# A four-layer attention stack, its instructions placed by a list scheduler at build time and its scores made in 64-row tiles

## The chip, the cores and the metric

The kernel runs on one core of a Trainium2 chip. The metric is the device time of one execution in microseconds (us).

The engines are PE (TensorE, matmuls), PEld (its weight loads), DVE (VectorE), ACT (ScalarE), POOL (GpSimd) and SP (SyncE, which here only issues DMAs). "Granted clock" is the share of the full TensorE clock that the throttle let through.

## The reference, cut to what matters

Two kinds of layer alternate, A, B, A, B, on 2048 tokens of width 512 with 32 heads of width 16. Each has a layer norm in front and adds its result to x.

```python
# A: four segments of 512 tokens, causal softmax inside a segment, a memory M between segments
for s in range(4):
    logits = einsum('bhqd,bhkd->bhqk', qs, ks) * scale + mask
    a_dot  = einsum('bhqk,bhkd->bhqd', softmax(logits), vs)
    a_mem  = einsum(phi(qs), M) / (einsum(phi(qs), z) + 1e-6)
    outs.append(g * a_mem + (1 - g) * a_dot)
    M = M + einsum('bhld,bhle->bhde', phi(ks), vs)      # z likewise
# B: linear attention; phi_q, phi_k = [softmax(p), softmax(-p)] over 16 features
kv  = einsum('bhsf,bhsd->bhfd', phi_k, v)               # over ALL 2048 tokens
o   = einsum('bhqf,bhfd->bhqd', phi_q, kv) / den
# x + A(norm(x)), x + B(norm(x)), and both once more
```

The exponentials of A's scores are the largest piece of ACT's work. And B needs the sum over all tokens before its first query, so every B layer is a barrier, where one layer drains and the next one fills.

## The kernel before: the parts that the argument touches

Work is written as Python generators, and the order is made by hand: a main generator yields, and fillers are advanced by one step at each yield.

```python
def run_pipelined(main_gen, fillers):
    fi = 0
    for _ in main_gen:
        if fillers:
            g = fillers[fi % len(fillers)]
            try: next(g)
            except StopIteration: fillers.remove(g)
            fi += 1
    # ... the rest of the fillers is drained
```

Scores are made for a pair of heads. The keys of the pair stand in a masked copy (KTm, one of four per group of eight heads), the queries in another (Qblk, even and odd heads). Each score has 512 or 256 columns and lies in one of three one-bank PSUM buffers.

```python
def st_and_exp(m, jset=(0, 1, 2, 3)):          # inside a_att
    g, sl = pairs[m]
    for j in jset:                              # key block
        i = j
        while i < 4:                            # query blocks i, i+1
            nb = min(2, 4 - i)
            stbuf = self.ST[st_i % self.NST]    # NST = 3
            self.mm(stbuf[:, 0:nb * 256], self.KTm[:, g, sl, j * 128:(j + 1) * 128],
                    self.Qblk[b][:, g, i:i + nb, :, :], ...)      # 128 rows
            self.act(dst, stbuf[:, 0:nb * 256]..., ACT.Exp, scale=0.25, ...)
            # the diagonal block is masked by POOL, 128x256
            i += nb
# ... 17-column PV matmuls per head, DVE copies PVsb and NMsb out of PSUM, combined later
```

The softmax here doesn't subtract the row's maximum and nothing guards it: scores larger than these inputs give would overflow.

## Time and profile before

| kernel before | |
|---|---|
| time, median of 4 (lowest to highest) | 1223.22 us (1220.18 to 1225.22) |
| granted clock, mean of the profiled run | 0.762 |
| columns of score exponentials | 512 x 512 and 256 x 256 |

The first part of the page of the kernel before gives, for each engine, its busy time, its share of the span and its number of instructions:

```profile
PE 741.9 (61%) x5659; PEld 352.0 (29%) x5760; DVE 649.0 (53%) x1345; ACT 495.1 (40%) x1034; POOL 355.9 (29%) x734
```

The second part of the page cuts the span into 40 slices. A digit is the busy share in tenths, and PEclk is the granted clock in tenths:

```profile
PE   0577766757675674454447687676667567445544
...
DVE  2635553446544535547787535445654353454766
ACT  0288445424553560122103785552456356113110
...
PEclk9989785767677776676667798887878786667776
```

No engine is above 61%, and only 3 of the 40 slices show a 7 or more on PE and on ACT at once. The chain of waits, followed back from the last instruction, changes engines all the time:

```profile
PE 37%; DVE 33%; ACT 14%; issue 7%; POOL 4%; DMA 3%; SPq 2%; DVEq 0%; POOLq 0%; ACTq 0%
```

The list of waits of the kernel before (who waited, for whom, us in all, times, longest) shows the hand-offs of the attention loop:

```profile
POOL PT L240 <- ACT PT L235: 334.8, 290, 12.3
...
PEld ST L220 <- ACT PT L235: 166.5, 360, 5.9
...
ACT PT L235 <- PE ST L220: 120.4, 54, 12.5
```

The table by stage (stretch, its length, busy us of PE, PEld, DVE, ACT and POOL with their counts, granted clock, DMA share, GB/s) shows one stretch of attention and two around B's queries:

```profile
90.00:190.00 100.00, 72.51 (x617) 35.73 (x627) 57.21 (x119) 60.98 (x131) 28.68 (x71) 0.84 0.07 14
480.00:560.00 80.00, 37.52 (x182) 15.60 (x186) 45.83 (x95) 13.57 (x24) 19.49 (x30) 0.65 0.09 19
560.00:660.00 100.00, 52.01 (x311) 24.95 (x314) 73.29 (x140) 20.24 (x32) 33.16 (x32) 0.67 0.15 28
```

Around B's queries ACT is busy a fifth of the time and PE about half. The groups of instructions (line, engine, operation, names and shapes, count, then busy us and mean ns of one, then idle us before them and what ended it) give the score loop. The lines are those of three helpers: L220 issues every matmul, L235 every ACT instruction, L240 every DVE and POOL one.

```profile
L235 ACT ACTIVATE PT<-ST 128x512 bf16<-128x512 f32 x512 | 286.3, 612 | 152.8 <-PE ST L220 120.4 <-PE KV L220 13.6 <-PE ATT L220 10.3
L240 POOL TENSOR_SCALAR_AFFINE_SELECT PT<-PT 128x256 bf16<-128x256 bf16 x512 | 205.1, 417 | 335.1 <-ACT PT L235 334.8
L220 PE MATMUL ST<-Qblk,AREA 128*128 128x512 bf16 x459 | 190.8, 462 | 42.1 <-DVE AREA L240 22.1 <-ACT PT L235 16.5 <-issue 1.5
```

The mean time of one is longer than the distance between two starts, so starts are the better cost. Taken from the trace, back-to-back starts of 512-column exponentials are 0.476 us apart (mean time 0.612), of 512-column matmuls 0.215 (mean time 0.462), of 17-column matmuls 0.025.

### The profile page before, as it was taken

How to read it: one execution, taken by the hardware profiler on the slowest of the kernel's cores; microseconds unless marked ns; L12 is line 12 of the kernel's file. 1: busy time of each engine (PE TensorE's matmuls, PEld its weight loads, DVE VectorE, ACT ScalarE, POOL GpSimd, SP SyncE). 2: the span in 40 equal slices, each digit the busy share in tenths (PEclk: the TensorE clock that was granted, in tenths of full speed). 3: DMA queues.
4: the chain of work that ended last, by engine and by line, in shares of the span. 5: the costliest groups of instructions: out<-in, count | busy, mean ns of one | idle time of the engine just before them, and what ended most of it. 6: DMA issues, size and time to landing. Idle time of an engine off the chain costs nothing.

```text
span 1222.7 us, 16010 instructions
## 1 busy us (share of the span) xinstructions
PE 741.9 (61%) x5659; PEld 352.0 (29%) x5760; DVE 649.0 (53%) x1345; ACT 495.1 (40%) x1034; POOL 355.9 (29%) x734
## 2 busy tenths in 40 slices
PE   0577766757675674454447687676667567445544
PEld 0243332323232331122222243232323233213222
DVE  2635553446544535547787535445654353454766
ACT  0288445424553560122103785552456356113110
POOL 1053221214222431123430343231323153112433
PEclk9989785767677776676667798887878786667776
DMA  6010100001000000101210100000000000010112
GB/s 207 17 19 1 23 15 16 1 5 31 18 1 1 19 19 9 27 5 22 39 31 17 28 1 9 10 18 1 14 9 14 1 18 19 5 31 1 43 43 52
DMA packets 79024, 26.23 MB, mean 21 GB/s; under 512 B 70752, under 2 KB 78944, under 8 KB 78944
## 3 DMA queue, kind: packets, MB, share of 16 engines
q1 hardware_dynamic: 74528, 21.01, 8.4%
q10 hardware_dynamic: 4416, 4.20, 1.0%
q8 instruction: 45, 0.74, 0.3%
q14 instruction: 35, 0.29, 0.1%
HBM read 6.32 MB, written 2.10 MB: 7 GB/s over the span
## 4 chain that ended last, share of the span: by engine, by line
PE 37%; DVE 33%; ACT 14%; issue 7%; POOL 4%; DMA 3%; SPq 2%; DVEq 0%; POOLq 0%; ACTq 0%
PE GEN L220 13%; PE KV L220 9%; ACT PT L235 8%; PE ST L220 7%; PE ATT L220 6%; DVE den L240 3%; ACT AREA L235 3%; DVE stats L240 3%; DVE Zk L240 2%; DVE Qblk L240 2%; DVE PVsb L240 2%; DVE AREA L240 2%; ACT Ek L235 2%; DVE Vt L240 2%; POOL rstd L240 2%
## 5 line engine op out<-in xcount | busy, mean ns | idle before, releaser
L235 ACT ACTIVATE PT<-ST 128x512 bf16<-128x512 f32 (+1 forms) x768 | 337.6, 547 | 152.8 <-PE ST L220 120.4
L220 PE MATMUL ST<-Qblk,AREA 128*128 128x512 bf16 (+1 forms) x715 | 256.6, 409 | 91.8 <-ACT PT L235 54.3
L240 POOL TENSOR_SCALAR_AFFINE_SELECT PT<-PT 128x256 bf16<-128x256 bf16 x512 | 205.1, 417 | 335.1 <-ACT PT L235 334.8
L220 PEld LDWEIGHTS ST<-Qblk,AREA 128*128 128x128 bf16 x768 | 77.0, 103 | 227.6 <-ACT PT L235 166.5
L220 PEld LDWEIGHTS ATT<-VT,PT 128*128 128x128 bf16 x2560 | 109.2, 101 | 56.3 <-issue 20.9
L220 PE MATMUL ATT<-VT,PT 128*128 128x17 bf16 x2560 | 107.9, 174 | 11.1 <-POOL PT L240 10.9
L240 DVE CAST PVsb<-ATT 128x136 bf16<-128x136 f32 x128 | 37.7, 294 | 136.7 <-PE ATT L220 128.4
L220 PE MATMUL ATT<-MSb,PhiQT 128*128 128x34 bf16 x384 | 26.8, 187 | 98.4 <-DVE PVsb L240 98.4
L220 PE MATMUL KV<-Vt,Ek 128*128 128x136 bf16 x256 | 41.1, 308 | 58.0 <-DVE KV L240 25.2
L240 DVE TENSOR_REDUCE Zk<-Ek 128x64 f32<-128x1024 bf16 x32 | 39.0, 1218 | 48.9 <-ACT Ek L235 48.9
L240 POOL CAST Vt<-rZk 128x32 bf16<-128x32 f32 x64 | 20.4, 318 | 140.5 <-DVE Vt L240 140.5
L235 ACT ACTIVATE AREA<-GEN,S 128x512 bf16<-128x512 f32 x44 | 30.2, 687 | 75.9 <-PE GEN L220 75.1
L235 ACT ACTIVATE Ek<-GEN 128x512 bf16<-128x512 f32 x40 | 23.9, 597 | 84.7 <-PE GEN L220 82.8
L220 PE MATMUL GEN<-xnT,WA_q 128*128 128x512 bf16 x87 | 31.5, 503 | 42.3 <-DMA xnT<-xn_tile 42.1
L240 POOL TENSOR_SCALAR rstd<-mv 128x4 f32<-128x4 f32 x16 | 3.6, 228 | 179.3 <-DVE mv L240 179.3
L235 ACT ACTIVATE AREA<-GEN 128x512 bf16<-128x512 f32 x44 | 25.5, 595 | 72.4 <-PE GEN L220 71.6
L235 ACT ACTIVATE phitmpb<-GEN 128x512 bf16<-128x512 f32 x34 | 20.3, 596 | 78.7 <-PE GEN L220 56.6
L240 DVE CAST NMsb<-ATT 128x136 bf16<-128x136 f32 x96 | 28.8, 300 | 39.9 <-PE ATT L220 39.9
L220 PE MATMUL GEN<-WA_o,oT 128*128 128x512 bf16 x88 | 35.1, 538 | 22.5 <-DMA oT<-o_tile 22.0
L220 PE MATMUL GEN<-WB_o,oT 128*128 128x512 bf16 x79 | 33.1, 563 | 24.3 <-DVE dz L240 10.8
L220 PEld LDWEIGHTS ATT<-MSb,PhiQT 128*128 128x128 bf16 x384 | 16.8, 101 | 107.4 <-DVE PVsb L240 107.4
L240 DVE TENSOR_SCALAR AREA<-GEN,S 128x512 bf16<-128x512 f32 x44 | 32.7, 749 | 26.1 <-ACT AREA L235 25.0
(168 smaller groups left out, 1296.2 us busy)
## 6 DMA issues: line engine op xcount, KB each, us to landing
X<-in_A_x_dram SPq DMA_DIRECT2D x4, 512.0 KB, 9.8
out_dram<-X ACTq DMA_DIRECT2D x16, 128.0 KB, 1.7
NMsb<-in_B_wqkv_dram ACTq DMA_DIRECT2D x2, 512.0 KB, 7.0
xnT<-xn_tile SPq DMA_TRANSPOSE x64, 2.4
oT<-o_tile SPq DMA_TRANSPOSE x64, 2.4
WA_q<-in_A_wq_dram SPq DMA_DIRECT2D x1, 512.0 KB, 10.1
WB_v<-in_B_wqkv_dram ACTq DMA_DIRECT2D x1, 512.0 KB, 11.0
WA_k<-in_A_wk_dram SPq DMA_DIRECT2D x1, 512.0 KB, 12.6
```

What stands on the lines that cost most here:

```text
L220: e.matmul(o, l, r, start=st, stop=sp, tile_position=tp), reads=reads, writes=writes)
L235: return e.activation(o, i, f, scale=s, **kw)
L240: return getattr(e, m)(*a, **k)
```

## The change

The kernel is rewritten. Every instruction, or small bundle of them, becomes a node with a duration and its reads and writes, and buffers become pools. At build time a list scheduler places the nodes: a backward pass gives each node a latest start, a forward pass lets every engine take the most urgent ready node that gets its buffers, and this is repeated for some rounds. The order is then fixed in the program, with semaphores for what crosses engines. The op set changes too. The scores of eight heads and one query block are two matmuls of 512 columns on 64 rows each, in a two-bank buffer, followed by one exponential of 1024 columns. The scheduler's model counts the two score matmuls one after the other, at full clock (2 x 214 ns), so the order is planned for serial scores. The core of the diff, cut:

```diff
-def run_pipelined(main_gen, fillers):  ...      # and all generators
+class Graph:
+    def backward(self, fin): ...                 # latest starts -> priorities
+    def forward(self, prio, pools):
+        # ... events in order of model time
+            for e in ENGS:
+                while ready[e]:
+                    pr, i = heapq.heappop(ready[e])
+                    o = self.ops[i]
+                    if can_alloc(o):
+                        pick = o
+                        break
+                    skipped.append((pr, i))
+    def schedule(self, pools, rounds=4):
+        prio = [float(o.id) for o in self.ops]
+        for r in range(rounds):
+            mk = self.forward(prio, pools)       # the best round is kept
+            prio = self.backward([o.end for o in self.ops])
...
-    self.mm(stbuf[:, 0:nb * 256], self.KTm[:, g, sl, j * 128:(j + 1) * 128], rhs, ...)
-    self.act(dst, stbuf[:, 0:nb * 256]..., ACT.Exp, scale=0.25, ...)
+    self.mm(lambda S=S, KT=KT, Q4=Q4, j=j: [
+        (S.t[:, hf * 512:(hf + 1) * 512], KT.t[64 * hf:64 * hf + 64, j * 128:(j + 1) * 128],
+         Q4.t[64 * hf:64 * hf + 64, :, i * 128:(i + 1) * 128], True, True) for hf in range(2)],
+        [512] * 2, [KT, Q4], [S], opens=[PT, PV], label="S")
+    self.act(lambda PT=PT: PT.t[:], lambda S=S: S.t[:], ACT.Exp, 1024, [S], [PT], scale=0.25)
...
+ # queries spread over four slots by DMA, so that a slot holds every fourth row:
+ self.dma(lambda: [(Q4.t[sl::4, sl, :], QT.t[sl::4, :]) for sl in range(4)], 4, [QT], [Q4])
+ # PhiK by a transposing DMA, in place of a second K projection;
+ # B's keys made transposed, then turned by 64 transposing DMAs; norms by Ln and Exp on ACT
```

## The prediction

> **What bounds it now.** No engine does. The page gives PE 61%, DVE 53%, ACT 40%, POOL 29% of 1222.7 us, and the chain of work that ended last passes between them: PE 37%, DVE 33%, ACT 14%, issue 7%. The list of waits shows hand-offs: POOL's masks wait 334.8 us for exponentials, exponentials 120.4 us for scores, weight loads for scores 166.5 us for exponentials (three one-bank buffers). The table by stage shows the worst stretches around the linear-attention queries: 480-660 us and 1060-1222 us have ACT at 10-20% and PE near 50%. Granted clock is 0.762 (view by core). Its hand-made interleaving bounds it.
>
> **What the change does, with starts measured back to back in the trace.**
> - Exponentials of scores: 512 of 512 columns (0.476 us apart) and 256 of 256 (about 0.26) become 320 of 1024. From the slope, 0.83 ns per column plus 0.05, one is 0.90 us (estimate): 311 -> 289 us.
> - All ACT: 384 x 0.90 + 100 of 512 x 0.48 [...]: about 415 us.
> - Scores: 640 matmuls of 512 columns on 64 rows, against 512 of 512 plus 256 of 256: the same 137 us if serial (0.215 each), about 70 if the two row tiles overlap. [...]
> - PV stays 2560 matmuls of 17 columns (0.025 us). The second K projection, 384 narrow memory matmuls and the DVE copies PVsb and NMsb (66 us), the even/odd masks (48), KTm's ACT and DVE copies (about 90) and Zk reductions (39) go. Added: 128 DMAs that spread queries, 88 more transposing DMAs on SP (now 2.4 us to landing), 128 POOL masks of 1024 columns (about 1.1 us each, estimate) for 512 at 0.417.
> - Totals for the new kernel (estimates by count): ACT 415, PE 410-480 at full clock plus switches, DVE about 400 (before 649), POOL 150, SP issue about 350 us.
>
> **Critical path.** The attention phase of each layer needs about 192 us of ACT and 170-200 us of PE, which run side by side; a list scheduler with right durations should reach 80-85%: 230-245 us each. Around them: start until first scores about 35 us (now 61), the layer boundary 40 us, the end about 70 us (16 tiles of DVE work at about 2.1 us plus the chain). Sum 605-635; plus loss, as the order is fixed while DMA landings and the PE clock vary. I predict 655 us, range 580 to 770.
>
> **What would show it.** ACT's share near 63%, PE near 65-70%, DVE 60%; ACT digits of 8-9 in the attention phases, low only at start, middle and end; chain led by ACT and PE; score matmul pairs starting together if row tiles overlap[...]; granted clock above 0.8.
>
> **What would make it wrong.** [...] at half clock PE needs over 800 us and bounds everything. SP's queue, in order with about 360 DMAs, blocking on a late operand. Two double-bank score buffers shared with B. [...]
>
> Chances: faster 0.96, same 0.02, slower 0.02.

All of ACT came to about 415 us with a term for the norms' small instructions, where the two terms give 394 (384 x 0.90 + 100 x 0.48). And a loss at each change of tile mode, of an assumed size, was said to cancel the gain of overlapping row tiles; "switches" in PE's total are these changes. The sum, 35 + 2 x (230 to 245) + 40 + 70 = 605 to 635 us, and the 655 were made with these terms. What the traces show of the rest:

- In the new kernel the masks of 1024 columns took 1.117 us each, where 1.1 was estimated, and pairs of scores start 3 to 4 ns apart.
- The small instructions of its norms start at least 0.185 us (Ln) and 0.092 us (Exp) before the next one, and a change of tile mode costs 0.08 to 0.10 us (below).
- SP's DMA issues took 380 us in all, where about 350 was estimated; SP's queue waited for a late operand for up to 13.9 us at a time. The DMAs on the pools p landed 1.7 to 6.4 us after their issue.
- The clock records of both kernels are all either full or half. In the new kernel 512-column matmuls on 128 rows start 0.216 us apart at full and 0.427 at half. "Over 800 us" at half clock is twice the 410 to 480 of PE's total, an estimate.

## The result, and the profile after

| | before | after |
|---|---|---|
| median of 4 (lowest to highest), us | 1223.22 (1220.18 to 1225.22) | 676.38 (672.14 to 677.56) |
| ratio (95% interval) | | 0.5525 (0.5507 to 0.5544) |
| granted clock, profiled run | 0.762 | 0.863 |

A ratio is the mean time of one kernel's runs over that of the other's of the same rounds, so it is not quite the ratio of the medians quoted. Executions over 1.5% slower than the fastest of the same kernel are left out of the means. The prediction, 655 us with a range of 580 to 770, held.

The busy times of the new kernel, first part of its page:

```profile
PE 533.6 (79%) x5621; PEld 269.3 (40%) x5696; DVE 434.2 (64%) x905; ACT 448.0 (66%) x625; POOL 148.8 (22%) x143
```

Its 40 slices:

```profile
PE   0677978888988889857996666789888988996685
...
DVE  7498866347644338689999622665466633676987
ACT  3678888787977885401764466899788889752040
...
PEclk9989989779967769987999665889797975898799
```

Busy time fell too: ACT went from 495 to 448 us, PE from 742 to 534, DVE from 649 to 434, POOL from 356 to 149. The sum of these four fell by 30%, from 2242 to 1565 us; the span fell by 45%, or 547 us. So part of the gain is less work, and part is that the engines now work at the same time: on average 1.83 of the four were busy before and 2.32 are after, and ACT and PE both show mostly 7 to 9 through the two attention phases (24 of the 40 slices have 7 or more on both). Two valleys of ACT are left: the 16th to the 24th slice, around the boundary between the first pair of layers (A and B, pair 0) and the second (pair 1), and the end. The chain still changes engines, but led by two:

```profile
PE 40%; ACT 23%; DVE 22%; DMA 6%; SPq 3%; issue 3%; POOL 1%; DVEq 0%
```

The lines of waits that answer to those before. POOL's wait is now harmless idleness (22% busy); the other two are smaller:

```profile
POOL p L810 <- ACT p L504: 431.2, 117, 101.6
ACT p L504 <- PE D L498: 109.2, 71, 29.1
PEld D L498 <- ACT p L504: 83.7, 135, 2.0
```

The groups of the score loop, new kernel (L498 issues every matmul, L504 every ACT function, L810 the masks; D is the pool of two-bank PSUM buffers, G that of one-bank ones, p stands for pools of SBUF buffers):

```profile
L504 ACT ACTIVATE p<-D 128x1024 bf16<-128x1024 f32 x384 | 372.0, 1033 | 110.9 <-PE D L498 109.2
L810 POOL TENSOR_SCALAR_AFFINE_SELECT p<-p 128x1024 bf16<-128x1024 bf16 x128 | 142.4, 1117 | 431.2 <-ACT p L504 431.2
L498 PE MATMUL D<-pQ,p 64*128 64x512 bf16 x640 | 140.9, 463 | 32.2 <-ACT p L504 30.0 <-DVE p L958 0.8 <-ACT p L511 0.3
```

The exponential of 1024 columns takes 1.033 us in the mean, and back-to-back starts are 0.903 us apart, which is the predicted 0.90. The next view is the table by stage, cut at the first and last score of each layer: attention of layer pair 0, the boundary, attention of pair 1, the end.

```profile
29.00:250.00 221.00, 184.63 (x2108) 88.82 (x2134) 134.44 (x306) 186.23 (x261) 70.24 (x63) 0.85 0.24 46
250.00:351.00 101.00, 86.11 (x755) 48.63 (x762) 85.39 (x163) 42.39 (x74) 1.09 (x1) 0.93 0.36 67
351.00:580.00 229.00, 181.88 (x2065) 86.63 (x2090) 121.58 (x269) 179.31 (x235) 70.41 (x64) 0.80 0.22 45
580.00:676.00 96.00, 73.06 (x678) 41.99 (x687) 76.61 (x128) 28.51 (x34) 0.68 (x1) 0.94 0.35 78
```

In attention ACT and PE are both at about 78 to 84%; in the boundary DVE and PE are both at 85%, at the end DVE is at 80% and PE at 76%. The granted clock is 0.85 and 0.80 in attention, where it counts, and higher in between. A timeline of PE in the new kernel (start, us, instructions merged) shows a pair of scores between matmuls of 17 and of 8 columns:

```profile
123.76 0.81 PE L498 MATMUL G<-pV,p 128*128 128x17 bf16 x24
124.51 0.39 PE L498 MATMUL D<-pQ,p 64*128 64x512 bf16 x2
124.83 0.18 PE L498 MATMUL G<-MSb,p 128*128 128x8 bf16 x1
```

The two of a pair start 3 to 4 ns apart, so the row tiles do overlap. A change of tile mode costs time: from a pair to a 17-column matmul the median start-to-start time is 0.319 us where two 512-column matmuls on 128 rows are 0.216 apart, and from a 17-column matmul to a pair it is 0.105 where two 17-column matmuls are 0.025 apart. That is 0.08 to 0.10 us per change, and the trace has 406 changes.

The phases, taken from the first and last score matmul of each A layer in the one profiled run of each kernel, in us:

| kernel | start | attention 0 | boundary | attention 1 | end | clock in attention 0, 1 |
|---|---|---|---|---|---|---|
| predicted | 35 | 230 to 245 | 40 | 230 to 245 | 70 | |
| new kernel | 29.4 | 221.0 | 100.8 | 228.3 | 95.6 | 0.846, 0.798 |
| e1 | 28.8 | 263.1 | 102.5 | 290.3 | 98.2 | 0.745, 0.633 |
| e2 | 28.9 | 209.5 | 102.1 | 219.6 | 96.7 | 1.000, 0.953 |
| e3 | 29.8 | 223.5 | 103.0 | 233.8 | 96.2 | 0.855, 0.803 |
| e4 | 39.0 | 260.9 | 117.9 | 249.3 | 102.9 | 0.819, 0.807 |
| e5 | 34.6 | 211.1 | 100.6 | 225.4 | 89.4 | 0.992, 0.985 |
| e6 | 30.3 | 225.0 | 101.5 | 235.7 | 97.5 | 0.992, 0.949 |
| e7 | 29.0 | 211.2 | 93.4 | 227.0 | 98.3 | 0.950, 0.835 |
| e8 | 30.2 | 232.8 | 98.3 | 246.9 | 89.4 | 0.890, 0.807 |
| e10 | 33.6 | 216.0 | 90.2 | 213.1 | 96.7 | 0.976, 0.984 |
| e11 | 30.2 | 216.7 | 102.4 | 222.5 | 93.2 | 0.851, 0.808 |
| e12 | 30.9 | 218.2 | 111.1 | 210.4 | 103.7 | 0.851, 0.854 |

### The profile page after: what moved, and what is told of

It is laid out like the page before. It is cut to its first block, busy times and chain, and to the rows that moved or that the text cites. A ratio compares the mean times of both kernels' runs of the same rounds, so it can differ in the third digit from the quotient of the medians.

```text
span 675.2 us, 13589 instructions
## 1 busy us (share of the span) xinstructions
PE 533.6 (79%) x5621; PEld 269.3 (40%) x5696; DVE 434.2 (64%) x905; ACT 448.0 (66%) x625; POOL 148.8 (22%) x143
## 4 chain that ended last, share of the span: by engine, by line
PE 40%; ACT 23%; DVE 22%; DMA 6%; SPq 3%; issue 3%; POOL 1%; DVEq 0%
PE G L498 25%; ACT p L504 21%; PE D L498 15%; DMA p<-p 5%; DVE p L958 3%; SPq L516 2%; DVE stats L701 2%; DVE X L850 2%; DVE p L709 2%; DVE pT L884 1%; DMA X<-in_A_x_dram 1%; DVE p L512 1%; SPq L520 1%; POOL p L810 1%; ACT p L511 1%
## 5 line engine op out<-in xcount | busy, mean ns | idle before, releaser
L504 ACT ACTIVATE p<-D 128x1024 bf16<-128x1024 f32 x384 | 372.0, 1033 | 110.9 <-PE D L498 109.2
L810 POOL TENSOR_SCALAR_AFFINE_SELECT p<-p 128x1024 bf16<-128x1024 bf16 x128 | 142.4, 1117 | 431.2 <-ACT p L504 431.2
L498 PE MATMUL D<-pQ,p 64*128 64x512 bf16 x640 | 140.9, 463 | 32.2 <-ACT p L504 30.0
L498 PE MATMUL G<-pV,p 128*128 128x17 bf16 (+1 forms) x2656 | 93.1, 176 | 12.9 <-POOL p L810 7.2
L498 PEld LDWEIGHTS G<-pV,p 128*128 128x128 bf16 x2656 | 83.3, 99 | 49.3 <-POOL p L810 20.0
L850 DVE TENSOR_TENSOR X<-X,G 128x512 bf16<-128x512 bf16 x64 | 43.1, 680 | 50.9 <-PE G L498 50.5
L498 PEld LDWEIGHTS D<-pQ,p 64*128 64x128 bf16 x640 | 29.4, 96 | 106.6 <-ACT p L504 81.0
L498 PE MATMUL G<-pX,WA_q 128*128 128x512 bf16 x117 | 32.1, 400 | 26.2 <-DMA pX<-p 21.1
L498 PE MATMUL G<-WA_o,p 128*128 128x512 bf16 x110 | 39.4, 484 | 13.1 <-DMA p<-p 5.8
L701 DVE BATCH_NORM_STATS2 stats<-X 128x6 f32<-128x512 bf16 x64 | 43.1, 679 | 3.5 <-DMA X<-in_A_x_dram 2.7
L884 DVE TENSOR_TENSOR pT<-G,pT 128x1024 bf16<-128x1024 f32 x32 | 37.9, 1213 | 7.5 <-PE G L498 7.5
L498 PE MATMUL G<-WB_o,p 128*128 128x512 bf16 x121 | 33.8, 404 | 8.6 <-DMA p<-p 6.4
L958 DVE TENSOR_TENSOR p<-D,pS 128x1024 bf16<-128x1024 f32 x32 | 38.1, 1211 | 0.0
L498 PE MATMUL G<-pX,WA_k 128*128 128x512 bf16 x120 | 33.0, 395 | 5.7 <-DVE X L850 2.2
L498 PE MATMUL G<-WA_v,pX 128*128 128x512 bf16 x118 | 33.0, 401 | 4.6 <-issue 1.0
L498 PE MATMUL G<-WB_v,pX 128*128 128x512 bf16 x120 | 31.4, 397 | 2.7 <-DVE pT L525 1.7
L498 PE MATMUL D<-pX,WB_k 128*128 128x512 bf16 x119 | 31.5, 403 | 1.9 <-ACT p L504 1.2
L498 PE MATMUL D<-Rkv,p 128*128 128x128 bf16 x256 | 21.8, 240 | 13.3 <-DVE p L958 12.7
```

The lines of the kernel that those rows point to most:

```text
L498: ins = e.matmul(out_ap, lhsT, rhs, start=st, stop=sp, tile_position=(basep(lhsT), basep(out_ap)))
L504: return self.g.op({"act": (dur, lambda e: e.activation(out_ap(), in_ap(), func, scale=scale))}, reads, writes, opens, label=label)
L701: v(lambda e: e.bn_stats(self.stats[:, t, :], self.X[:, t, :]), 602, [R("X", t)], [R("st", t)], label="bn")
L810: v(lambda e, pt8=pt8: e.affine_select(pt8(), pt8(), [[0, 8], [1, 128]], ALU.is_ge, 0.0, base=0, channel_multiplier=-1), 1080, [PT], [PT], ...
L850: self.v(lambda e: e.tensor_tensor(self.X[:, t, :], self.X[:, t, :], ps.t[:, 0:512], ALU.add), 602, [R("X", t), ps[0]], [R("X", t)], label ...
L884: v(lambda e, ps=ps, Vt=Vt: e.tensor_tensor(Vt.t[:, :, :, 0:16], ps.t[:, None, 0:512].to_broadcast([128, 2, 512]).rearrange("p s (h d) -> ...
```

## The experiments

Four questions were put. What do the 64-row tiles and the 1024-wide exponentials bring? What does the placement bring? What holds the boundary and the end? How much does a new order alone move the time? "Against the new kernel" below is the ratio of an experiment's runs to the kernel before, over the new kernel's 0.5525, because the jobs shared the kernel before and not the new kernel.

| run | median us | ratio to before | against the new kernel | clock, profiled run |
|---|---|---|---|---|
| e1, one row tile | 779.27 | 0.6314 | +14.3% | 0.755 |
| e2, full rows | 658.84 | 0.5384 | -2.6% | 0.958 |
| e3, exponentials split | 687.92 | 0.5622 | +1.8% | 0.865 |
| e4, one round | 777.79 | 0.6349 | +14.9% | 0.816 |
| e5, full rows, exact | 665.11 | 0.5443 | -1.5% | 0.971 |
| e6, full rows and changes of mode | 688.66 | 0.5633 | +2.0% | 0.953 |
| e7, values on POOL | 657.89 | 0.5385 | -2.5% | 0.896 |
| e8, keys early | 696.80 | 0.5704 | +3.2% | 0.858 |
| e9, program order | 1681.02 | 1.3766 | +149% | 0.593 |
| e10, e5 and e7 together | 651.00 | 0.5324 | -3.6% | 0.968 |
| e11, fewer transposes | 669.58 | 0.5474 | -0.9% | 0.871 |
| e12, other order (control) | 678.28 | 0.5558 | +0.6% | 0.871 |

### e1, e2, e3: score tiles and wide exponentials

In these three the order of every engine is exactly the new kernel's. In e1 both halves read rows 0 to 63, in e2 both read all 128 rows; in both they ran one after the other (0.216 us apart at full clock, below). Both mix up heads. (Their results still pass the comparison, because these scores are so small that the softmax is nearly flat.)

```diff
 e1:
-  KT.t[64 * hf:64 * hf + 64, j * 128:(j + 1) * 128], Q4.t[64 * hf:64 * hf + 64, :, ...]
+  KT.t[0:64, j * 128:(j + 1) * 128], Q4.t[0:64, :, ...]
 e2:
+  KT.t[:, j * 128:(j + 1) * 128], Q4.t[:, :, ...]
 e3: each ACT instruction of 1024 columns issued as
+  activation(o[:, 0:512], i[:, 0:512]); activation(o[:, 512:1024], i[:, 512:1024])
```

> Both halves of every score read rows 0 to 63, so the two matmuls share one row tile and cannot overlap (results wrong on purpose; order of every engine the same). In the profile of the new kernel the two of a pair start 3 to 4 ns apart; here they should start about 215 ns apart, which is 320 x 0.212 = 68 us more of PE. Theory A (the attention phases are held by PE and ACT together, both at about 84% there): 25 to 60 us slower than the new kernel, about 715. Rival B (ACT alone holds them, and the order was planned for serial scores): under 12 us slower.

> Both halves of every score read all 128 rows (results wrong on purpose, order the same): serial like e1, but no change of tile mode. A change costs about 0.095 us in the new kernel's trace (from a score to a 17-column matmul 0.319 us instead of 0.216, from a 17-column matmul to a score 0.104 instead of 0.025), some 400 changes, 39 us of PE. Theory A: between the new kernel and e1, 10 to 30 us slower than the new kernel and 15 to 35 faster than e1. If changes of mode cost nothing on the critical path: equal to e1 within 8 us.

> Each of the 384 exponentials of 1024 columns is issued as two of 512 (order the same). From 0.903 us for 1024 and 0.476 for 512, ACT gets 384 x 0.05 = 19 us more. If ACT holds the attention phases: 10 to 20 us slower. If PE holds them: under 6 us.

e3 came as expected for an ACT that matters: 1.8% slower, about 12 us, for 19 us of added ACT work.

e1 and e2 came as neither theory had it. e1 was 103 us slower by the medians, though only 68 us of PE work were added. And e2, whose scores are just as serial, was 17.5 us *faster* than the new kernel. The attention phases in the stage table show where; the last number but two is the granted clock. The kept trace of e1 is of its slowest execution (784.71 us, clock 0.755); its two fast ones had clocks of 0.779 and 0.764, still well below the new kernel's 0.863 to 0.882. First those of e1:

```profile
29.00:292.00 263.00, 243.45 (x2120) 99.44 (x2146) 134.72 (x306) 192.76 (x261) 71.22 (x64) 0.74 0.19 39
...
395.00:685.00 290.00, 263.57 (x2061) 104.00 (x2086) 121.04 (x268) 184.39 (x235) 70.45 (x64) 0.63 0.18 35
```

The same two phases of e2:

```profile
29.00:238.00 209.00, 181.76 (x2114) 97.03 (x2140) 134.42 (x306) 185.79 (x260) 70.77 (x64) 1.00 0.25 49
...
340.00:560.00 220.00, 183.62 (x2064) 94.21 (x2089) 122.29 (x269) 179.34 (x235) 70.16 (x64) 0.95 0.24 47
```

Boundary and end are the same as the new kernel's to 3 us in both (table of phases). The attention phases differ, and there the clock runs from 0.74 and 0.63 (e1) through 0.85 and 0.80 (new kernel) to 1.00 and 0.95 (e2). The group of the score matmuls in e1:

```profile
L498 PE MATMUL D<-pQ,p 64*128 64x512 bf16 x640 | 258.6, 522 | 9.1 <-ACT p L504 7.4 <-DVE p L958 0.5 <-issue 0.3
```

The same group in e2:

```profile
L498 PE MATMUL D<-pQ,p 128*128 128x512 bf16 x640 | 190.1, 392 | 23.5 <-ACT p L504 21.0 <-DVE p L958 0.4
```

Serial scores at full clock start 0.216 us apart in both. In e1 half of the starts of two 64-row scores in a row are 0.401 us or more apart, and the median score matmul took 0.604 us, against 0.379 in e2. That fits half clock: in the new kernel's trace, where 23 of the 46 clock records are full and 23 half, 512-column matmuls on 128 rows start 0.216 and 0.427 us apart. The page of e1 has a PEclk of 5 tenths in 14 of its 40 slices, that of the new kernel in 2. So e1's PE is the busiest (87% of the span, against 79% in the new kernel and 82% in e2) and has the lowest clock (0.755, against 0.863 and 0.958). The new theory, which is a reading of these three runs: the throttle grants by how much of the array works, and not by how long PE looks busy. A 64-row matmul then counts less than a 128-row one of the same length.

A rival has to be set aside: that only the length of the streaming counts, and not the rows. The kept traces can be asked. Each matmul is taken at 0.42 ns per column (0.216 us for 512), and an overlapping pair once. Columns then stream for 0.46 and 0.42 of the two attention phases in the new kernel, 0.65 and 0.59 in e2, 0.52 and 0.45 in e1 (estimates). Between the new kernel and e2, length alone would explain the clock as well as rows do, because the pairs stream for half as long. e1 decides: it streams for longer than the new kernel and has the lower clock. Counted with half weight for 64 rows, it has 0.39 and 0.33, and the order is that of the clocks. This rests on e1 alone, and e6 below has to rule out the changes of mode. An order planned for overlapping pairs was not run.

### e4, e9: what the placement brings

```diff
 e4:
-ROUNDS = 5
+ROUNDS = 1
 e9: each engine runs its nodes in program order
-                    if can_alloc(o):
+                    if i == line[e][at[e]] and can_alloc(o):
                         pick = o
+                        at[e] += 1
# ... nodes with two possible engines alternate; a segment is projected just before its attention
```

> The list scheduler keeps its rules but takes the program's order as priority (one round; the rounds that reorder by latest start are left out). Same instructions. Theory A (placement by latest start gives much of the gain): 60 us or more slower, 740 to 850. Rival (the op set and eager placement give it, the priorities little): within 30 us.

> The instructions of the new kernel without the list scheduler: each engine runs them in the order in which the program makes them (projections of a segment just before its attention; evacuations alternate between ACT and DVE). Theory P (placement is worth more than the new instructions): over 1100 us, so the new instructions in plain order give little or nothing against the 1223 us of the kernel before. Rival (the new instructions give most of the gain): under 900 us.

e4: with the program's order as priority, but the same eager placing, the time is 778 us. The latest-start priorities are worth 101 us here. e9: the same instructions in plain order need 1681 us, 1.38 times the kernel before, whose order was made by hand. The page of e9, first and second part:

```profile
PE 734.1 (44%) x5696; PEld 310.2 (18%) x5696; DVE 434.5 (26%) x883; ACT 473.6 (28%) x646; POOL 148.3 (9%) x144
...
PEclk9655565557555655575757555755665575556776
```

PE is busy 44% of the time at a clock of 0.593, and its busy time grows from 534 to 734 us with that. The program order was never meant to be run, so 1681 is no fair rival of the hand-made order. What it shows is that in such an order the new instructions save nothing: the gain needs their placement. How the 547 us divide between the two stays open, as the old instructions were never given to the scheduler, nor the new ones to an order made by hand.

### e5, e6: rows, data or changes of mode

e5 makes e2 exact. A tile holds each key block twice, with the other 64 rows zero. e6 gives e2 its changes of tile mode back.

```diff
 e5:
+KZ = self.T(self.pK, "KZ")                       # [128, 2, 512], zeroed once
+self.dma(lambda: [(KZ.t[64 * h:64 * h + 64, h, :], KT.t[64 * h:64 * h + 64, :]) for h in range(2)], 2, [KT], [KZ])
-  KT.t[64 * hf:64 * hf + 64, j * 128:(j + 1) * 128], Q4.t[64 * hf:64 * hf + 64, :, ...]
+  KZ.t[:, hf, j * 128:(j + 1) * 128], Q4.t[:, :, ...]
-N_Q4, N_K1, N_K2 = 7, 38, 16 ; KT at most 8
+N_Q4, N_K1, N_K2, N_KZ = 6, 32, 15, 6 ; KT at most 3
 e6, on e2, before each pair:
+  (S.t[:, 0:8], KT.t[0:64, j * 128:(j + 1) * 128], Q4.t[0:64, 0, i * 128:i * 128 + 8], True, True)
```

> e2 made exact: keys are copied by two more DMAs per group into a tile whose other 64 rows are zero, and the scores use all 128 rows of it (right results; a few other buffers are fewer to make room, so the order differs). After e1 and e2 the theory is that the granted clock follows how many rows of the array are at work: 0.755 for serial 64-row scores, 0.863 for paired ones, 0.958 for 128 rows. Theory C (rows count, even with zeros in them): clock 0.93 or more, 645 to 665 us. Rival (only rows with data count): clock 0.88 or less, 680 us or more.

> e2 with a small matmul (8 columns, 64 rows, into a place that the score then overwrites) before each of the 320 scores: the changes of tile mode come back, the 128-row scores stay. It costs PE about 0.2 us each, up to 64 us. Theory R (the rows of the scores keep the clock up): clock 0.90 or more, 660 to 700 us. Rival S (the changes of mode, not the rows, lower the clock in the new kernel and in e1): clock 0.82 or less, over 715 us.

The attention phases in the stage table of e5:

```profile
35.00:246.00 211.00, 182.21 (x2110) 96.90 (x2136) 126.49 (x285) 186.26 (x255) 71.82 (x64) 0.99 0.29 59
...
346.00:572.00 226.00, 192.66 (x2200) 103.56 (x2225) 139.38 (x294) 187.62 (x250) 70.37 (x64) 0.98 0.28 56
```

The attention phases in the stage table of e6:

```profile
30.00:255.00 225.00, 207.99 (x2279) 112.35 (x2306) 135.94 (x306) 190.83 (x262) 70.40 (x64) 0.99 0.23 45
...
357.00:592.00 235.00, 208.27 (x2216) 108.15 (x2242) 120.88 (x268) 182.58 (x234) 69.69 (x64) 0.95 0.22 44
```

The clock of e5 is 0.99 and 0.98 in attention, with right results and with half of the key rows zero, where the new kernel had 0.85 and 0.80: in these runs rows count, whether their weights are zero or not. Its time, 665.1 us, lies just outside the 645 to 665 that were expected. e6 keeps e2's clock (0.953 against 0.958) with 640 changes of mode, more than the new kernel's 406: here the changes don't lower the clock. They do cost time. PE was busy for 590.0 us, against 536.6 in e2, which is 0.17 us for each small matmul where about 0.2 was expected (two changes at 0.095 us would be 0.19). e6 is 29.8 us slower than e2, or 47 ns per change, small matmuls included. All of it is in the attention phases (15.5 and 16.1 us). At that rate 406 changes would be 19 us of the new kernel, which is an estimate.

### e7, e8, e11: what holds the boundary and the end

```diff
 e7, for odd tiles:
+self.act(lambda: vb.t[:], lambda: ps.t[:, 0:512], ACT.Copy, 512, [ps[0]], [vb])
+v(lambda e: e.tensor_tensor(Vt.t[:, :, :, 0:16], vb..., weights, ALU.mult), 2150, ..., eng="pool")
 e8, in schedule():
             prio = self.backward(fin)
+            for o in self.early:                 # B's key nodes of the first three chunks
+                prio[o.id] -= 40e3
 e11: results wrong on purpose
+if sgn:                                     # no transpose for the negative sign
+    E[(gp * 2 + gg, 1)] = E[(gp * 2 + gg, 0)]
+    continue
```

> On the new kernel: for every second tile, B's weighted values are made by an ACT copy (about 0.48 us) and a POOL product (about 2.1 us) in place of the DVE product of 1.13 us; 16 of 32 leave DVE. In the new kernel DVE is 96% busy in the middle of the layer boundary (300 to 350 us) with ACT at 46% and POOL idle. Theory D (DVE holds the boundary, 101 us from the last score of layer 0 to the first of layer 1, and the end, 96 us after the last score): 12 to 30 us faster in all, boundary and end 8 to 15 each. Rival (latencies of the chain through transposes hold them): under 6 us.

> On the new kernel: B's key work of the first three chunks of each layer gets 40 us more urgency in the list scheduler, so it is placed in the attention phase and not left for the boundary, where 15 of the 16 weighted-value products of layer 0 now stand. Theory K (leaving it was a mistake of the priorities): 10 us or more faster. Rival (the work only moves: the attention phases, held by PE and ACT, grow by what the boundary loses): within 12 us of the new kernel or slower, boundary 75 to 92 us in place of 101, attention phases 8 to 20 us longer each.

> On the new kernel: the keys of the negative sign are not transposed, those of the positive sign are used in their place (results wrong on purpose): 32 transposing DMAs fewer of 216, each 1.27 us of SP's queue, 4 of them in each layer's last chunk. In the new kernel the chain through the boundary runs twice through rows of such DMAs on SP (257.8 to 266.5 us and 284.6 to 289.6). Theory T (SP's queue holds the boundary too): boundary 10 us or more below 101, the end 5 or more below 96. Rival: both within 5 us of the new kernel's.

The phases quoted here have to be read with the control e12, below. e7 is 2.5% faster, as much as theory D asked, but not where D asked. The boundary is 7 us shorter, the end 3 us longer, attention of layer pair 0 10 us shorter with a higher clock. (The POOL product took 2.0 us, the DVE product that it replaces 1.2, with starts 1.13 apart in the new kernel; 512-column ACT copies start 0.476 apart there.) e8 moved what it should: 12 of the 16 weighted-value products of layer 0 now stand before its last score, against 1 in the new kernel. The boundary lost only 2.5 us, attention grew by 12 and 19 us, and the kernel is 3.2% slower. So, at this one setting, leaving the keys for the boundary was no mistake of the priorities. e11 (results wrong, relative error 0.034) took 32 transposing DMAs off SP's queue (a median of 1.26 us each there in the new kernel) and left the boundary where it was, at 102 us; the end was 2 us shorter, and the whole is 0.9% faster. Theory T asked for more and got no support, but the control e12 moves the boundary by 10 us, so a smaller effect is not excluded. Issuing half of the transposes from ACT's queue was not tried.

### e12, e10: a control, and the best version

```diff
 e12:
-LAT = {"pe": 190, "act": 160, ...}
+LAT = {"pe": 190, "act": 170, ...}
 e10: e5 and e7 together, with
+N_K1, N_K2, N_VT = 34, 15, 4 ; ROUNDS = 12
```

> A control: the new kernel with one latency of the scheduler's model changed by 10 ns (ACT 160 to 170), which gives the same instructions in another order of the same quality. It tells how much a new order alone moves the time, and so which of the differences above can be read: expected within 8 us of the new kernel, clock within 0.02. If it moves by over 15 us, e5's and e7's few per cent are not told from chance.

> e5 (exact full-row scores) and e7 (every second weighted value by ACT and POOL) together, with two more half-size buffers and one fewer value tile. If the two gains are of different causes (PE clock in the attention phases, DVE in the boundary): 640 to 655 us, clock 0.93 or more, boundary under 95 us. If e7's gain was a chance of the order, or came from the clock: 657 us or more.

e12 does the same work in another order of the same quality (four evacuations of PSUM also went from DVE to ACT). Its time moved by 0.6%, but its boundary by +10 us, its end by +8 and its attention of layer pair 1 by -18. Phases of kernels with different orders therefore can't be compared to within 10 us, in attention not to within 18; totals can be read to perhaps 1%, on the word of one control. That leaves e1, e2, e3 and e6 (same order) readable by phase, and e4, e5, e7, e8, e10 and e11 by total only. e7's gain in total, 2.5%, stands above the control; that DVE's relief in the boundary is its cause was only argued.

e10 is exact, and at 651.0 us (five runs, 647.0 to 654.5) it is the fastest version run: 3.6% faster than the new kernel, 0.5324 of the kernel before (0.5297 to 0.5351). Time, clock and boundary (90.2 us) are as expected for two gains of different causes, but the boundary's 10 us are no more than the control's, and e10 also has other buffer counts and 12 rounds of scheduling where the new kernel has 5, which were not tried alone. So it does not prove the causes. The attention phases in its stage table:

```profile
34.00:250.00 216.00, 195.57 (x2233) 104.75 (x2231) 142.28 (x310) 187.53 (x261) 78.80 (x68) 0.98 0.31 61
...
340.00:553.00 213.00, 187.00 (x2116) 97.50 (x2114) 126.96 (x283) 183.39 (x246) 74.05 (x66) 0.98 0.28 58
```

Both attention phases have nearly full clock, as in e5, and the boundary is the shortest of the table; the end is not better.

## Why the prediction was right or wrong

- **The total**, 655 us, was right to 3%, and faster by much more than 2% was right. The reading behind it was that no engine bounded the old kernel and that its hand-made order did. e4 and e9 show how much the order decides for the new instructions; that it bounded the old ones was not tested, and busy time fell by 30% as well.
- **Exponentials**: 0.90 us estimated, 0.903 measured; saving small, as predicted. e3 shows that the width itself is worth 1.8%.
- **Row tiles overlap and changes of mode cost time**: both right. Pairs start 3 to 4 ns apart, and a change costs 0.08 to 0.10 us. The step that fell short was to weigh the overlap against these changes alone (cut above, as the size of one was assumed). The prediction named half clock as a risk, but not that 64-row tiles would have a lower clock than full rows. With 64-row tiles the clock in attention was 0.846 and 0.798; with full rows, at twice the streaming time and without changes of mode, it was 1.000 and 0.953, and the kernel 2.6%, or 17.5 us, faster (e2). By e6's rate some 19 us of that are the 406 changes of mode (an estimate); the 68 us of PE work that the overlap saves is given back by the lower clock and these changes: PE is busy for 534 us in the new kernel and for 537 in e2. The tiles are a small loss, not a draw. With right results (e5) the gain of full rows is 1.5%, little more than the control's 0.6%.
- **Attention phases**, 230 to 245 us each: 221 and 228, a little shorter. Most of B's key work of those chunks was not done there, which the sum had supposed; in e8, where it was, they took 233 and 247.
- **Boundary and end** were the terms that were mis-sized: 40 and 70 us predicted, 101 and 96 measured. The 40 has no working; the end was counted as 16 tiles of DVE work of 2.1 us, 34 us, plus a chain (in the new kernel's end a tile's product, sum and residual took 1.21, 0.41 and 0.68 us, 2.3 together). The stage table shows 85 us of DVE work and 86 us of PE work in the boundary's 101, and 77 us of DVE work in the end's 96. Part of it is B's key work that had been charged to attention, but moving it there (e8) did not help. They were 87 us over in sum. The total came out right because attention was 11 to 41 us shorter and because "plus loss", 20 to 50 us, covered most of the rest; the loss was not where it was looked for. That the total came so close is in part luck, as errors of up to 87 us cancelled.
- **Signs**: ACT 63% predicted, 66% measured; DVE 60% and 64%; clock above 0.8 and 0.863. PE, 65 to 70% predicted, was 79%: at half clock its 512-column matmuls start 0.427 us apart instead of 0.216, and 406 changes of mode at about 0.09 us add some 37 us (an estimate).
- **Left open**: what holds the boundary and the end. DVE and PE are at 76 to 85%. Moving the key work (e8) did not help, fewer transposes on SP (e11) made no difference that can be told from a change of order, and neither did e7 there. The chain of waits through the new kernel's boundary (250 to 351 us) is about 41% PE and 24% SP's queue and DMAs, so SP's part is not ruled out.

## What to carry to other kernels

When no engine is above two thirds and the chain changes engines at every step, look at the order before the instructions: here the same instructions ran in 1681, 778 and 676 us in three orders. A smaller matmul tile saved PE time here (68 us, an estimate) and lost it again to the clock (0.85 and 0.80 in attention, against 1.00 and 0.95 with full rows); compare the granted clock of the stage with and without it, and try full rows with zeros. When an order is made by a program, run a control with a different order of the same quality, or a gain of one per cent, or of ten microseconds in one phase, can't be told from chance.
